# Another order of loads, stores, scores and out products in a fused attention and feed-forward kernel

## The chip, the core and the metric

The kernel runs on one core of a Trainium2 chip. The metric is the device time of one execution in microseconds (us); lower is better. Engines are named as the profile names them: PE is TensorE (its weight loads stand apart as PEld), DVE is VectorE, ACT is ScalarE, POOL is GpSimd, and SP is SyncE, whose queue issues nearly every transfer here.

## What is computed

A linear attention with a decay per head (4 batches, 8 heads, 768 positions, head size 64) is followed by a bilinear feed-forward layer over the 3072 tokens (512 wide, 1536 inside). The reference works in blocks of 64 positions with a running state; the kernel uses blocks of 128.

```python
for b in range(nb):                       # per batch and head
    intra = einsum('bhic,bhjc->bhij', qb, kb) * Dmask
    intra = einsum('bhij,bhjd->bhid', intra, vb)
    inter = einsum('bhid,bhde->bhie', qb * lam_pow, kv_state)
    out[:, :, sl] = intra + inter
    kv_state = lam_block * kv_state + einsum('bhsd,bhse->bhde', kb * rev_pow, vb)
x = out.transpose(0, 2, 1, 3).reshape(3072, 512)
y = ((x @ w_a) * (x @ w_b)) @ w_out       # 512x1536, 512x1536, 1536x512
```

## The kernel before, in words

**Units and groups.** A unit is 128 tokens of one batch with all heads: 24 units, six to a batch. Units 0 to 3 are packed and handled ahead of the loop. The feed-forward part takes the units in eight groups, `GROUPS = (4, 1, 2, 4, 4, 4, 4, 1)`: group 1 is unit 4 alone, group 2 is units 5 and 6, group 3 is units 7 to 10, group 4 units 11 to 14. While group g goes through the feed-forward products, the attention of later units is worked in between.

**Slots.** What is worked in between is written out by hand in `PLAN` (lines 42 to 81): per group a list of (slot, step, unit). The feed-forward code calls `hook(slot)` at fixed points, and each call issues the steps of that slot. Instructions stand on every engine's queue in the order of this program; nothing reorders them. The steps that matter here:

- `PK`, `PV`, `P` (prep, lines 423 to 436): scale k and then q of a unit into one bf16 tile `qk` (line 401; POOL from unit 6 on), and cast v to `vb` (line 420; the engine is listed in `VB_ENG`). For units 7 and up (`DMA_T`) prep also issues a transposing transfer `qkT<-qk` on SP (line 429). Units 4 to 6 are transposed on PE instead (`T`, lines 438 to 446), with a copy on ACT (line 445). After v, `pump()` (line 302) issues the loads of the units that the look-ahead now allows.
- `S` (scores, lines 451 to 482): eight small matmuls `kq<-qkT` (line 457), then two masks on DVE (line 480), or one on DVE and one by way of ACT (lines 471 and 472).
- `O2` (line 571): for two units the products with the state and with the values into `o_ps` (line 497), copied to `xT` by ACT (line 520), and the state update `kvd` (lines 527 and 549). `V` (line 566) is a state update by itself, with a copy into `st` (line 560).
- `W` (line 627): issues one store on SP of a row of results that was kept in SBUF. The five rows of groups 0 and 1 are kept (`o_kept`, line 634) in tiles of `snap_pool`, which has seven buffers. The same pool holds the tiles `u` of line 829, snapshots of PSUM that the feed-forward of groups 3 to 6 needs.
- `WS` (line 260): eight sums of weights, 128x1536 each, ready before group 3 uses them as `wz_a`, `wz_b`. `WS_ENG` names the engine: DVE for 0 to 6 and POOL for 7.
- `X`, `XA`: sums of xT on DVE ahead of group 3 (lines 708 to 722).

**Feed-forward.** Groups 0, 1, 2 and 7 use the plain form (`ffn`): 12 passes of an `a_ps` and a `b_ps` product (line 596), a copy of a on ACT (line 605), the product ab on DVE (line 623); `hook(0)` to `hook(11)` stand behind these passes. Then come, per unit, 12 out products `op<-wo_sb,ab` (line 643), six ahead of a hook and six behind it; then the store and one more hook. Groups 3 to 6 use a form with seven products in place of eight (`ffn_z`, line 748), six passes with three hooks each; its snapshots `u` on ACT and sums `oab` on DVE (lines 777 to 789) stand between products on PE. In group 3 the out products (line 810) follow in `out_plain`, with the hooks 18 to 25.

**Loads.** `pending` (lines 292 to 299) lists all loads in order, for every unit q, k, v. All go through SP's queue in program order, with three buffers each for q, k and v.

Of the kernel before, what the change touches and what calls it, by code (L numbers as in the profile page):

```python
# [22 lines left out]
def _bc(ap, dims):  # L23
# [9 lines left out]
DMA_T = range(7, 24)  # L33
# [71 lines left out]
                        ["act"] * 3))  # L105
SUM_ENG = {(3, 0): 'dve', (3, 1): 'dve', (3, 2): 'pool', (3, 3): 'dve', (3, 4): 'pool', (3, 5): 'pool', (3, 6): 'dve', (3, 7): 'dve', (4, 0): 'dve', (4, 1): 'pool', (4, 2): 'pool', (4, 3): 'pool', (4, 4): 'dve', (4, 5): 'pool', (4, 6): 'pool', (4, 7): 'pool', (5, 0): 'dve', (5, 1): 'dve', (5, 2): 'pool', (5, 3): 'pool', (5, 4): 'dve', (5, 5): 'pool', (5, 6): 'pool', (5, 7): 'dve', (6, 0): 'pool', (6, 1): 'dve', (6, 2): 'pool', (6, 3): 'dve', (6, 4): 'dve', (6, 5): 'pool', (6, 6): 'dve', (6, 7): 'dve'}
XS_ENG = {(3, 0): 'dve', (3, 1): 'dve', (3, 2): 'dve', (4, 0): 'dve', (4, 1): 'dve', (4, 2): 'dve', (5, 0): 'dve', (5, 1): 'pool', (5, 2): 'pool', (6, 0): 'pool', (6, 1): 'pool', (6, 2): 'pool'}
WS_ENG = {0: 'dve', 1: 'dve', 2: 'dve', 3: 'dve', 4: 'dve', 5: 'dve', 6: 'dve', 7: 'pool'}
WO_ENG = {0: 'dve', 1: 'dve', 2: 'pool', 3: 'dve', 4: 'dve'}
CO_ENG = {0: 'pool', 1: 'pool', 2: 'pool', 3: 'dve', 4: 'dve', 5: 'dve'}  # L110

# [2 lines left out]
def kernel(  # L114
# [12 lines left out]
    B, H, S, D = q.shape  # L127
# [3 lines left out]
    d_model, d_ff = moe_w_a.shape  # L131
# [4 lines left out]
    FC = d_ff // 128  # L136
# [123 lines left out]
    def weight_sum(i):  # L260
# [5 lines left out]
        a21, a22 = w[:, 0:2, HF:], w[:, 2:4, HF:]  # L266
        eng = eng_of(WS_ENG[i])
        if j == 0:
# [23 lines left out]
    pending = []  # L292
# [3 lines left out]
    pending += [("o", c) for c in range(4)] + [("q", n0), ("k", n0)]  # L296
    pending += [("o", 4), ("o", 5), ("v", n0)]
    for u in range(n0 + 1, NU):
        pending += [("q", u), ("k", u), ("v", u)]
    used = {"u": 0}  # L300

    def pump():
# [36 lines left out]
    for w, src in (("q", q), ("k", k)):  # L339
# [3 lines left out]
        for c in range(0, HP, n_c):  # L343
            if w == "q":
                t = oab_pool.tile([128, 1024], F32, name="q4", tag="oab")
            else:
                t = snap_pool.tile([128, 512], F32, name="k4", tag="snap")
            t = t[:].rearrange("p (c b x) -> p c b x", c=n_c, b=2)
# [48 lines left out]
    def eng_of(name):  # L397
        return nc.gpsimd if name == "pool" else nc.vector
# [136 lines left out]
    def kv_update(u):  # L535
        if u % NB == NB - 1:
            return
        if u % NB == 0:
            kv_bank()
        kv_mms(kv["ps"], u, range(HP), u % NB == 0)  # L540
# [22 lines left out]
    def piece_S(u):  # L563
        masks(u, scores(u))
# [43 lines left out]
    def a_part(f, xT, gt):  # L608
        return a_copy(half(wa_sb, f, xT, "a_ps", 0, gt), gt)

    def a_parts(fs, xT, gt):
        ps_parts[0] = True
        pss = [half(wa_sb, f, xT, "a_ps", 0, gt // 2) for f in fs]
        a_sbs = []
        for f, ps in zip(fs, pss):
            half(wa_sb, f, xT, "a_ps", gt // 2, gt, ps)
            a_sbs.append(a_copy(ps, gt))
        ps_parts[0] = False
        return a_sbs

    def b_part(f, xT, gt, a_sb, ab):
        ps = half(wb_sb, f, xT, "b_ps", 0, gt)
        nc.vector.tensor_mul(ab[:, f, :gt], a_sb[:, :gt], ps[:, :gt])  # L623
# [7 lines left out]
    def store(row, op, lo, hi, queue=None):  # L631
        if row < g_u0[KEEP_GROUPS]:
            o_sb = snap_pool.tile([128, d_model], F32, name="o_kept", tag="snap")
            nc.scalar.copy(o_sb, op)
            kept.append((row, o_sb))
            return
        o_sb = o_pool.tile([128, d_model], F32, name="o_sb", tag="osb")
        nc.scalar.copy(o_sb[:, lo:hi], op[:, lo:hi])
        (queue or nc.sync).dma_start(out=out_r[row][:, lo:hi], in_=o_sb[:, lo:hi])

    def out_mms(op, ab, t, fs, lo=0, hi=d_model):
        for f in fs:
            nc.tensor.matmul(op[:, lo:hi], lhsT=ab[:, f, t * 128:(t + 1) * 128],  # L643
                             rhs=wo_sb[:, f, lo:hi], start=(f == 0), stop=(f == FC - 1))

    def ffn(u0, n, xT, hook, first, last):
        gt = n * BLK
        ab = ab_pool.tile([128, FC, 512], BF16, name="ab", tag="ab")
        if first:
            for i, cs in enumerate(W_STEPS):  # L650
                nxt = W_STEPS[i + 1] if i + 1 < len(W_STEPS) else ()
                fs = range(w_off[cs[0]] // 128, w_off[cs[-1] + 1] // 128)
                a_sbs = a_parts(fs[:2], xT, gt) if i == 0 else []
                a_sbs += [a_part(f, xT, gt) for f in fs[len(a_sbs):]]
                if i == 0:
                    kv_update(n0 - 1)
                    cast_w("b", cs[1], "both")
                else:
                    for c in nxt:
                        cast_w("a", c, "dve")  # L660
                for n_f, (f, a_sb) in enumerate(zip(fs, a_sbs)):
                    b_part(f, xT, gt, a_sb, ab)
                    hook(f)
                    if i == 0 and n_f == 1:
                        cast_w("a", nxt[0], "dve")
                for c in nxt:
                    cast_w("b", c, "act")
            ops = [ps_bank("op", [128, d_model], F32, hold=True) for _ in range(n)]
            slot = FC
            for c in range(FC // 2):  # L670
                for t in range(n):
                    out_mms(ops[t], ab, t, range(2 * c, 2 * c + 2))
                    if c == FC // 2 - 1:
                        store(u0 + t, ops[t], 0, d_model)
                    hook(slot)
                    slot += 1
            bank["held"].clear()
            return
        for f in range(FC):
            a_sb = a_part(f, xT, gt)  # L680
            b_part(f, xT, gt, a_sb, ab)
            hook(f)
        for t in range(n):
            op = ps_bank("op", [128, d_model], F32, ffn=True)
            if last and t == n - 1:
                for lo, hi in ((0, 256), (256, 384), (384, 512)):
                    if lo:
                        op = ps_bank("op", [128, d_model], F32, ffn=True)
                    out_mms(op, ab, t, range(FC), lo, hi)
                    store(u0 + t, op, lo, hi, nc.scalar if hi == d_model else None)  # L690
                return
            out_mms(op, ab, t, range(FC // 2))
            hook(FC + 2 * t)
            out_mms(op, ab, t, range(FC // 2, FC))
            store(u0 + t, op, 0, d_model)
            hook(FC + 2 * t + 1)
# [318 lines left out]
    for g, n in enumerate(GROUPS):  # L1015
# [6 lines left out]
        def hook(slot, plan=plan):  # L1022
            for name, us in plan.get(slot, ()):
                if name == "C":
                    cast_w("o", us, CO_ENG[us])
                elif name == "PK":
                    prep_k(us)
                elif name == "PV":
                    prep_v(us)
                elif name == "P":  # L1030
                    prep_k(us)
                    prep_v(us)
                elif name == "W":
                    store_kept()
                elif name == "WS":
                    weight_sum(us)
                elif name == "WO":
                    out_sum(us)
                elif name == "SM":
                    ab_sum(*us)  # L1040
                elif name == "H":
                    out_half(*us)
                elif name == "XA":
                    x_add_first(us)
                elif name == "X":
                    x_sums(us)
                elif name == "T":
                    piece_T(us)
                elif name == "S":
                    piece_S(us)  # L1050
                elif name == "VC":
                    kv_copy(us, kv["ps"], KV_ENG[us])
                elif name == "V":
                    piece_V(us)
                elif name == "O":
                    pieces_O((us,))
                elif name == "O2":
                    pieces_O(us)
                else:
                    pieces_O(us[:2], us[2:])  # L1060
# [41 lines left out]
```

## Time and profile before

| what | value |
|---|---|
| median of 3 runs | 224.38 us (224.23 to 226.21) |
| time of the profiled execution | 223.83 us |
| span of the profiled execution (first to last instruction) | 222.1 us |
| PE busy | 213.9 us (96%) |
| DVE, ACT, POOL busy | 165.3, 122.7, 99.8 us |
| transfers | 39.42 MB; read 28.32 MB, written 6.29 MB |
| granted TensorE clock | 1.000 over the span |

The span is 1.7 us shorter than the time of the same execution; the rest lies before the first and behind the last instruction. A busy PE need not be PE at its pace: matmuls are pipelined, so a wait shows best as the distance between the starts of two neighbours. All places are in us from the start of the span.

### The profile page before, as it was taken

The page shows a single profiled execution, that of the slowest core. Times are in us where ns is not written, and L with a number is a line of the kernel's source. Part 1 is how long each engine was busy: PE and PEld are TensorE (multiplying, and loading weights), DVE is VectorE, ACT ScalarE, POOL GpSimd, SP SyncE. Part 2 cuts the span into 40 slices and gives each one's busy share as a digit, 9 for nine tenths or more (in the row PEclk, how much of TensorE's full clock was granted, in tenths as well). Part 3 has the DMA queues.
Part 4 walks back from the last instruction along what each step waited for, and adds up shares of the span by engine and source line. Part 5 has one row for each costly group of instructions (what it writes and reads, how often), then busy time and mean ns, then how long its engine had stood idle before and what let it go on. Part 6 is the DMA issues. An engine that isn't in the chain of part 4 may idle for free.

```text
span 222.1 us, 5601 instructions
## 1 busy us (share of the span) xinstructions
PE 213.9 (96%) x2225; PEld 159.0 (72%) x2235; DVE 165.3 (74%) x272; ACT 122.7 (55%) x249; POOL 99.8 (45%) x95
## 2 busy tenths in 40 slices
PE   7899999999999999999999999899999999999994
PEld 2476444448678657787547888688888888888994
DVE  0994773968798668889888889968688865777540
ACT  3686446038454266775356988776535666543322
POOL 6061004246795175540559559786417722051100
PEclk9999999999999999999999999999999999999999
DMA  4999999999999999999999999652021100112042
GB/s 132 321 265 349 356 387 344 277 216 218 216 204 220 232 174 248 190 275 245 180 248 236 233 201 211 138 101 50 0 88 56 52 0 4 47 47 97 0 145 94
DMA packets 99081, 39.42 MB, mean 177 GB/s; under 512 B 85488, under 2 KB 95088, under 8 KB 99056
## 3 DMA queue, kind: packets, MB, share of 16 engines
q1 hardware_dynamic: 98768, 39.00, 79.8%
q8 instruction: 17, 0.28, 0.6%
q10 hardware_dynamic: 288, 0.07, 0.1%
q14 instruction: 8, 0.07, 0.1%
HBM read 28.32 MB, written 6.29 MB: 156 GB/s over the span
## 4 chain that ended last, share of the span: by engine, by line
PE 67%; DMA 16%; SPq 5%; DVE 5%; ACT 2%; issue 2%; POOL 1%; ACTq 0%; DVEq 0%; POOLq 0%
PE U L748 17%; PE op L870 12%; PE V L748 9%; DMA wst<-in_moe_w_b_dram 8%; PE b_ps L596 5%; PE op L810 5%; PE a_ps L596 5%; PE W L748 4%; PE op L643 3%; DMA kf<-in_k_dram 3%; DMA k<-in_k_dram 3%; PE o_ps L497 3%; PE kq L457 2%; DMA out_dram<-o_kept 2%; SPq L187 1%
## 5 line engine op out<-in xcount | busy, mean ns | idle before, releaser
L829 ACT COPY u<-U 128x512 f32<-128x512 f32 x48 | 28.3, 590 | 16.5 <-PE U L748 16.4
L401 POOL TENSOR_TENSOR qk<-kf,lp_k 128x512 bf16<-128x512 f32 x18 | 19.5, 1084 | 33.7 <-DMA kf<-in_k_dram 18.9
L623 DVE TENSOR_TENSOR ab<-a_sb,b_ps 128x128 bf16<-128x128 bf16 (+2 forms) x48 | 19.2, 417 | 13.6 <-ACT a_sb L605 10.2
L596 PE MATMUL a_ps<-xT,wa_sb 128*128 128x128 bf16 (+2 forms) x198 | 27.6, 267 | 0.5 <-DVE wa_sb L244 0.2
L480 DVE TENSOR_TENSOR m<-kq,lotri 128x512 bf16<-128x512 f32 x40 | 25.6, 682 | 3.1 <-PE kq L457 3.0
L596 PE MATMUL b_ps<-xT,wb_sb 128*128 128x128 bf16 (+2 forms) x192 | 27.5, 272 | 0.2
L756 DVE TENSOR_TENSOR ab<-oab 128x1024 bf16<-128x1024 bf16 x24 | 19.0, 791 | 11.3 <-ACT oab L754 11.1
L401 POOL TENSOR_TENSOR qk<-qf,lp_q 128x512 bf16<-128x512 f32 x20 | 24.8, 1242 | 1.7 <-DMA qf<-in_q_dram 1.7
L605 ACT CAST a_sb<-a_ps 128x128 bf16<-128x128 f32 (+2 forms) x48 | 17.3, 374 | 14.7 <-PE a_ps L596 14.4
L643 PE MATMUL op<-wo_sb,ab 128*128 128x512 bf16 (+2 forms) x114 | 21.8, 334 | 0.5 <-issue 0.3
L596 PEld LDWEIGHTS <-wa_sb 128*128 128x128 bf16 x200 | 16.7, 98 | 6.6 <-issue 0.5
L748 PEld LDWEIGHTS <-wz_a 128*128 128x128 bf16 x192 | 18.2, 98 | 3.9 <-issue 0.9
L748 PEld LDWEIGHTS <-wz_b 128*128 128x128 bf16 x192 | 18.7, 98 | 2.2
L596 PEld LDWEIGHTS <-wb_sb 128*128 128x128 bf16 x192 | 15.8, 98 | 6.2 <-issue 0.2
L748 PE MATMUL U<-xT,wz_a 128*128 128x256 bf16 x96 | 18.3, 272 | 0.0
L748 PE MATMUL U<-xT,wz_b 128*128 128x256 bf16 x96 | 18.3, 272 | 0.0
L520 ACT CAST xT<-o_ps 128x512 bf16<-128x512 f32 (+1 forms) x24 | 12.2, 554 | 10.7 <-PE o_ps L497 10.5
L787 DVE TENSOR_TENSOR oab<-U,u 128x512 bf16<-128x512 f32 x24 | 16.3, 681 | 0.8 <-PE U L748 0.8
L420 POOL CAST vb<-vf 128x512 bf16<-128x512 f32 x14 | 10.2, 730 | 13.8 <-DMA vf<-in_v_dram 13.8
L748 PEld LDWEIGHTS <-wa_sb 128*128 128x128 bf16 x144 | 13.4, 98 | 4.0 <-issue 1.0
L643 PEld LDWEIGHTS <-ab 128*128 128x128 bf16 x120 | 10.1, 98 | 8.5
L754 ACT CAST oab<-U 128x512 bf16<-128x512 f32 x24 | 14.2, 592 | 3.5 <-PE U L748 3.5
(130 smaller groups left out, 453.1 us busy)
## 6 DMA issues: line engine op xcount, KB each, us to landing
vf<-in_v_dram SPq DMA_DIRECT2D x24, 256.0 KB, 4.9
qf<-in_q_dram SPq DMA_DIRECT2D x20, 256.0 KB, 4.6
kf<-in_k_dram SPq DMA_DIRECT2D x20, 256.0 KB, 4.7
out_dram<-o_sb SPq DMA_DIRECT2D x18, 256.0 KB, 2.4
wst<-in_moe_w_a_dram SPq DMA_DIRECT2D x6, 512.0 KB, 8.8
wst<-in_moe_w_b_dram SPq DMA_DIRECT2D x6, 512.0 KB, 9.2
wst<-in_moe_w_out_dram SPq DMA_DIRECT2D x6, 512.0 KB, 10.7
out_dram<-o_kept SPq DMA_DIRECT2D x5, 256.0 KB, 4.3
```

The costliest lines, as they stand in the source:

```text
L401: eng_of(eng).tensor_mul(dst.rearrange("p (c b) d -> p b c d", b=2), x[:].rearrange("p (b c) d -> p b c d", b=2), lp.rearrange("p (b c) o ...
L480: nc.vector.tensor_mul(m, kq[i], lotri_bc)
L596: nc.tensor.matmul(ps[:, lo:hi], lhsT=w_sb[:, s, f * 128:(f + 1) * 128], rhs=xT[:, s, lo:hi], start=(s == 0), stop=(s == KS - 1), skip_gro ...
L605: nc.scalar.copy(a_sb[:, :gt], ps[:, :gt])
L623: nc.vector.tensor_mul(ab[:, f, :gt], a_sb[:, :gt], ps[:, :gt])
L643: nc.tensor.matmul(op[:, lo:hi], lhsT=ab[:, f, t * 128:(t + 1) * 128], rhs=wo_sb[:, f, lo:hi], start=(f == 0), stop=(f == FC - 1))
L748: nc.tensor.matmul(ps[:, k, :], lhsT=wt[:, s, n * 128:(n + 1) * 128], rhs=rhs[i][:, s, :], start=(fresh and k == 0 and s == 0), stop=True, ...
L754: nc.scalar.copy(oab[:, 0], U)
L756: nc.vector.tensor_mul(ab[:].rearrange("p (h i) (t c) -> p h i t c", h=2, t=2)[:, :, n], o5[:, :, :, 0, :], o5[:, :, :, 1, :])
L787: nc.vector.tensor_sub(oab[:, 1], U, v1)
L829: nc.scalar.copy(t, ps)
L870: nc.tensor.matmul(ps[:, t, :], lhsT=lhs[p][:, n, t * 128:(t + 1) * 128], rhs=rhs[:, n, :], start=fresh, stop=True, skip_group_check=True)
```

## The change

In `PLAN`, the sums of weights 5, 6 and 7 move from group 1's slots 0 and 13 to group 1's slot 13 and group 2's slots 9 and 13, and sum 7 moves from POOL to DVE. The transposes of unit 6 now stand ahead of the scores of unit 5. Of the five stores of kept rows, the third moves up behind the first two in group 2's slot 2, and the last two move to group 3's slot 21. The scores of units 11 and 12 and the `O2` behind them move one slot later. The load list has k ahead of q for units 7 to 23. In `ffn`, the 12 out products of a group of one unit are issued as four, hook 12, four, hook 13, four, store; this branch runs for unit 4 alone, since unit 23 leaves by the branch above it.

```diff
     1: [
-        (0, 'PV', 5), (0, 'WS', 5), (3, 'T', 5), (4, 'PK', 6), (6, 'PV', 6), (9, 'P', 7),
-        (11, 'S', 5), (11, 'T', 6), (12, 'S', 6), (13, 'P', 8), (13, 'O2', (5, 6)), (13, 'V', 6),
-        (13, 'WS', 6), (13, 'WS', 7)],
+        (0, 'PV', 5), (3, 'T', 5), (4, 'PK', 6), (6, 'PV', 6), (9, 'P', 7),
+        (11, 'T', 6), (11, 'S', 5), (12, 'S', 6), (13, 'P', 8), (13, 'O2', (5, 6)), (13, 'V', 6), (13, 'WS', 5)],
     2: [
-        (2, 'W', None), (2, 'W', None), (3, 'P', 9), (4, 'V', 7), (4, 'S', 7),
-        (6, 'V', 8), (10, 'PK', 10), (11, 'PV', 10), (11, 'P', 11), (11, 'W', None),
+        (2, 'W', None), (2, 'W', None), (2, 'W', None), (3, 'P', 9), (4, 'V', 7), (4, 'S', 7),
+        (6, 'V', 8), (9, 'WS', 6), (10, 'PK', 10), (11, 'PV', 10), (11, 'P', 11),
         (11, 'S', 8), (11, 'P', 12), (12, 'Q', (7, 8, 9, 10)), (13, 'P', 13),
-        (13, 'W', None), (13, 'V', 9), (14, 'XA', 3), (14, 'O2', (9, 10)), (14, 'X', 3), (15, 'W', None)],
+        (13, 'V', 9), (13, 'WS', 7), (14, 'XA', 3), (14, 'O2', (9, 10)), (14, 'X', 3)],
     3: [
-        (1, 'S', 11), (5, 'S', 12), (8, 'O2', (11, 12)), (10, 'P', 14), (12, 'S', 13),
+        (2, 'S', 11), (6, 'S', 12), (9, 'O2', (11, 12)), (10, 'P', 14), (12, 'S', 13),
...
-        (19, 'P', 16), (19, 'O2', (13, 14)), (20, 'P', 17), (21, 'S', 15), (21, 'P', 18),
+        (19, 'P', 16), (19, 'O2', (13, 14)), (20, 'P', 17), (21, 'S', 15), (21, 'P', 18), (21, 'W', None), (21, 'W', None),
...
-WS_ENG = {0: 'dve', 1: 'dve', 2: 'dve', 3: 'dve', 4: 'dve', 5: 'dve', 6: 'dve', 7: 'pool'}
+WS_ENG = {0: 'dve', 1: 'dve', 2: 'dve', 3: 'dve', 4: 'dve', 5: 'dve', 6: 'dve', 7: 'dve'}
...
     for u in range(n0 + 1, NU):
-        pending += [("q", u), ("k", u), ("v", u)]
+        pending += [("k", u), ("q", u), ("v", u)] if u in DMA_T else [("q", u), ("k", u), ("v", u)]
...
+            if n == 1:
+                out_mms(op, ab, t, range(4))
+                hook(FC)
+                out_mms(op, ab, t, range(4, 8))
+                hook(FC + 1)
+                out_mms(op, ab, t, range(8, FC))
+                store(u0 + t, op, 0, d_model)
+                return
             out_mms(op, ab, t, range(FC // 2))
             hook(FC + 2 * t)
```

In the program's order on SP, the two late stores stand behind the loads of unit 20 and ahead of the last two row stores of group 3 and the transposing transfer of unit 19. Every engine keeps its instructions, but for sum 7, which leaves POOL's queue for DVE's.

6 rows, old and new, of the table PLAN are left out of this document.

## The prediction

> **What bounds the kernel.** I read the page first, then PE's waits, then the chain of waits, then the timeline wherever two neighbours on PE start too far apart.
>
> ```profile
> span 222.1 us, 5601 instructions
> ...
> PE 213.9 (96%) x2225; PEld 159.0 (72%) x2235; DVE 165.3 (74%) x272; ACT 122.7 (55%) x249; POOL 99.8 (45%) x95
> ```
>
> PE is the bound: busy for 96% at a granted clock of 1.000, with neighbouring matmuls of 128, 256 and 512 columns 56, 109 and 216 ns apart. The change removes no matmul, so it can only win where PE waits. PE's own list of waits is short:
>
> ```profile
> PE U L748 <- DVE oab L787: 0.8, 1, 0.8
> ...
> PE V L748 <- ACT u L829: 0.3, 1, 0.3
> ```
>
> The first stands at 141.20, where group 4 ends, and no edit touches it. The second is on the chain:
>
> ```profile
> 83.72 4.32 DMA out_dram<-o_kept
> 88.11 0.59 ACT u L829
> 88.75 0.60 PE V L748 x4
> ```
>
> The third kept row is stored from 83.72 on, lands at 88.03, and only then may ACT's snapshot take its buffer; PE stood behind the snapshot. The list shows 0.3 because it counts a matmul's modelled end; from start to start it is 0.61 where 0.11 is usual: 0.50 lost.
>
> The list shows no shorter wait. Two places on the timeline do. In group 1:
>
> ```profile
> 52.48 1.39 DVE L273 TENSOR_TENSOR wz_b<-wb_sb,wz_b 128x1536 bf16<-128x1536 bf16 x1
> ...
> 53.80 0.67 DVE L623 TENSOR_TENSOR ab<-a_sb,b_ps 128x128 bf16<-128x128 bf16 x3
> ...
> 54.13 0.38 PE L596 MATMUL b_ps<-xT,wb_sb 128*128 128x128 bf16 x4
> ```
>
> Weight sum 5 keeps DVE until 53.8; the products behind it free a PSUM bank late, and PE starts `b_ps` at 54.13, 0.33 behind its neighbour instead of 0.06: 0.27 lost. At the end of group 1:
>
> ```profile
> 60.71 3.09 POOL L275 TENSOR_TENSOR wz_b<-wb_sb 128x1536 bf16<-128x1536 bf16 x1
> 61.39 2.70 DVE L420 CAST vb<-vf 128x512 bf16<-128x512 f32 x1
> ...
> 61.58 0.58 ACT L634 COPY o_kept<-op 128x512 f32<-128x512 f32 x1 [2.01 <-PE op L643]
> ...
> 62.17 1.07 ACT L520 CAST xT<-o_ps 128x512 bf16<-128x512 f32 x2
> ...
> 62.28 0.40 PE L527 MATMUL kvd<-vb,qk 128*128 128x128 bf16 x4
> ...
> 62.80 0.87 PE L596 MATMUL a_ps<-xT,wa_sb 128*128 128x256 bf16 x4
> ```
>
> ACT copies `o_kept` ahead of the two halves of xT, and group 2's first product waits for each half: 0.35 instead of 0.06, then 0.38 instead of 0.11. That is 0.29 + 0.27 = 0.56 lost.
>
> **The change, part by part.**
>
> *Sum 5 leaves group 1's slot 0.* DVE reaches the products 1.39 earlier, and the 0.27 goes. Next to be late would be unit 6's transposes, which now stand first in slot 11: in the kernel before they could start when POOL had scaled q of unit 6 (57.34) and started at 57.90. Without the 0.27 and with unit 5's scores (0.33) behind them, PE wants them at 57.90 - 0.33 - 0.10 - 0.27 = 57.20. If POOL keeps its times, 0.14 or a little more is given back. But POOL's scale at 53.02 took 1.75 beside sum 5, where others take 1.04; without the sum it should be some 0.7 earlier. I take -0.27, bounds -0.27 to -0.10.
>
> *Transposes first, out products in three parts.* The copy `qkT` (1.01 on ACT, begun 0.2 after the last transpose) is ready near 58.9; unit 6's scores want it at 57.20 + 0.45 + 0.33 + 4 x 0.216 + 0.10 = 59.0. Four products more (0.87) bring `O2` at 60.35; unit 6's masks (two, 1.29, from 0.43 behind its scores) end near 60.8 and are wanted near 60.9. `O2` and the state update take 0.80 + 0.23, and the last four products (0.87) bring PE to 62.24, when both halves of xT are copied (near 62.15), since `o_kept` now comes behind them. So the 0.56 goes. `o_kept` ends near 63.0; its bank is wanted by the second `a_ps` at 63.1. Three margins are about 0.1 each: bounds -0.56 to -0.30, and I take -0.56, since each is a margin and not a deficit. Scores and `O2` cost 0.1 each on either side where PE changes to small tiles; their number is the same.
>
> *Third kept store sooner.* It is issued at about 68.7 in place of 83.72 and lands, at the 3.9 to 4.5 us of its kind, near 73, 14 us before its buffer is wanted: -0.50, and behind it the snapshot waits for PE alone. Price: SP's issue (0.36 to 1.10 in the rows) delays what is queued behind: transposing transfers of units 9 and 10 (8 us early for their scores at 76.26), loads of 11 and 12, transfer 11.
>
> *Two later.* The last two leave 95.28 and 96.89 on SP for the place behind unit 20's loads. Their buffers: in the kernel before, group 3's snapshots already turned over in the other five until pass 5; now for pass 5 too. The five sufficed for passes 1 to 4 with no wait of DVE or ACT on a buffer after 88; 0, bounded by one snapshot (0.59). Queued behind them are two row stores and the transfer of unit 19: below.
>
> *k ahead of q.* The 34 loads of units 7 to 23 swap places on SP, two by two. POOL waited 18.9 us in seven waits for kf; it now starts with the load that lands 1.2 us earlier, scales k while q lands, and ends a pair about 1.0 sooner. PE gets nothing: every transposed tile had landed before its scores. Tightest was unit 11 (issued 79.26, landed 84.22, scores 84.85), then 12 (89.00 for 89.77), 19 (131.07 for 132.87).
>
> *Scores 11 and 12 one slot later.* Eight matmuls, two masks and, with `O2`, one state update move past two products (0.87). Unit 11's scores then fall at 84.85 - 0.83 + 0.87 = 84.9. Its transfer: +0.36 to +1.10 for the third store, -0.6 for POOL; its landing 83.6 to 84.7. No wait, bounds 0 to +0.5. `O2` comes one slot nearer to unit 13's scores (3 us of products between), its copies (1.07) fit.
>
> *Sums 5, 6, 7 in their new places.* Sum 5 takes DVE where sum 6 did (1.19). Sum 6 (0.95 to 1.39) falls where DVE idled 0.45 in each pass; unit 8's masks then end up to 0.4 later, where 0.49 was spare before `O2` needed their banks. Sum 7 falls ahead of group 3's sums of xT, where DVE idled 1.59 waiting for ACT's xT at 82.07. POOL is rid of 3.09 us, and the cast beside it (2.70; 0.42 at 67.17) of 2.3. All 0.
>
> [...]
>
> **Sum.** -0.27 - 0.56 - 0.50 = -1.33 us. The profiled execution took 223.83: 222.50 after. Its time lies 0.55 under the median of the runs shown, 224.38; on that scale 223.05, so **223.1 us**.
>
> **Rivals.**
>
> *Unit 11's transfer lands late.* If POOL's gain fails and the store costs SP its 1.10, it lands at 84.22 + 1.10 = 85.3; PE, due at 84.9, waits 0.5: 223.6.
>
> *Sum 7 waits for POOL.* If it loses two scales (2 x 1.04) to POOL, DVE is late by 0.95 + 2.08 - 1.59 = 1.44 for group 3's sums. `z_add` ended 0.76 before its product and the moved scores take 0.33 of that: PE loses 1.0, 224.1. Against it: no DVE row shows two such waits in a row.
>
> *The waits come back later*, at 141.20, and nothing is won: 224.4. Against it: that wait's chain (ACT oab, DVE ab, zab, oab) begins at PE's own products, so it moves with PE.
>
> *Slower: the two late stores hold up unit 19.* In the kernel before its transfer was issued at 125.62 and landed at 131.07; PE now wants its scores at 132.87 - 1.33 = 131.54. If the two stores cost SP 1.10 each and nothing has been won ahead of them, it lands at 133.3: PE waits 1.7, ends at -1.33 + 1.7 = +0.4, 224.8. It turns to slower once unit 19 lands after 132.9. For it: SP waits at 112.67 for a row copied by ACT, so what SP gains from the three stores taken away (1.03 + 1.10 + 0.45) may be lost there. Against it: that row comes 1.33 earlier too, and transfers drain in the meantime.
>
> **Chances.** Sum as worked out 0.66; unit 11 late 0.12; sum 7 behind POOL 0.08; waits come back 0.07; unit 19 late 0.07. The likeliest alone spans 222.5 to 223.6 (the bounds that give back 0.17 + 0.26 + 0.1 on the high side, 0.5 from the wait at 141 or from POOL on the low one). The range 222.4 to 224.8 takes in the third and fourth and reaches to the slower case; it leaves out half of that and the tails: under 2 in 10. About 1% is what a measurement of this kernel can tell from no change: below 222.1 is 0.04 (tail of the first case), above 226.6 is 0.02 (unit 19 with more behind it), within 0.94.
>
> **What would show it.** Right: `b_ps` of pass 4 in group 1 follows 0.06 behind its neighbour; group 2's `a_ps` runs four at 0.11; no ACT wait on `o_kept`; the span near 220.8; PE's list keeps only the wait on oab L787. Wrong: a wait of PEld L457 on a transposing transfer (unit 11 or 19), `o_ps` waiting for a mask in group 1, V's or W's products waiting for DVE at 82 to 86, or a larger wait at 141.

## The result, and the profile after

| | kernel before | changed kernel |
|---|---|---|
| median of 20 executions | 224.16 us (223.50 to 226.21) | 226.18 us (223.42 to 231.32) |
| ratio, without the longest executions | 1 | 1.0044 (95%: 1.0023 to 1.0066) |
| time of the profiled execution | 223.83 us | 225.38 us |
| its span | 222.1 us | 223.6 us |

By the ratio the change made the kernel about 0.4% slower, 1 us; 223.1 us had been forecast. The ratio leaves out executions more than 1.5% above the fastest of their kernel, which are nine of the changed kernel's twenty and none of the kernel before's, while the medians count all and lie 2.0 us (0.9%) apart.

From the page of the changed kernel, its span and its busy time by engine:

```profile
span 223.6 us, 5612 instructions
...
PE 212.8 (95%) x2225; PEld 158.6 (71%) x2235; DVE 167.7 (75%) x273; ACT 122.3 (55%) x249; POOL 97.7 (44%) x94
```

PE has the same 2225 matmuls and a longer span: it waits more. First the three places that the change aimed at. Group 1 on the timeline (start, us, engine, line, operation):

```profile
54.12 0.39 PE L595 MATMUL a_ps<-xT,wa_sb 128*128 128x128 bf16 x4
54.34 0.39 PE L595 MATMUL b_ps<-xT,wb_sb 128*128 128x128 bf16 x4
```

Four products every 0.22: the 0.27 at `b_ps` is gone. The end of group 1:

```profile
61.52 1.07 ACT L519 CAST xT<-o_ps 128x512 bf16<-128x512 f32 x2 [2.17 <-PE o_ps L496]
...
61.87 1.03 PE L642 MATMUL op<-wo_sb,ab 128*128 128x512 bf16 x4
...
62.73 0.60 PE L595 MATMUL a_ps<-xT,wa_sb 128*128 128x256 bf16 x4
62.93 0.58 ACT L633 COPY o_kept<-op 128x512 f32<-128x512 f32 x1 [0.34 <-PE op L642]
...
63.17 0.60 PE L595 MATMUL b_ps<-xT,wb_sb 128*128 128x256 bf16 x4
```

ACT copies both halves of xT while PE works on the last third of the out products; `o_kept` comes behind them; the next four `a_ps` take 0.44, 0.11 each. The 0.56 is gone. And the third kept store, issued at 69.27, landed at 73.29; PE's list of waits has no snapshot behind a store any more. But beside the wait on `oab` that was there before it has a new line:

```profile
PE U L755 <- ACT u L836: 1.3, 2, 1.1
```

The chain of waits (start, us, what) says where it is and what is behind it:

```profile
84.61 0.59 ACT u L836
85.25 0.60 PE U L755 x4
...
134.89 0.44 ACT u L836
135.37 0.60 ACT oab L761
136.03 5.91 DMA vf<-in_v_dram
142.01 0.48 issue
142.48 0.59 ACT u L836
143.12 0.61 PE U L755 x4
```

The load of v of unit 22, issued at 136.03, lands at 141.94. ACT's cast of it stands on ACT's queue ahead of a snapshot, and PE waits for the snapshot. The same two instructions on the timeline, with what ended the idle time ahead of them in brackets:

```profile
141.96 0.62 ACT L417 CAST vb<-vf 128x512 bf16<-128x512 f32 x1 [2.86 <-DMA vf<-in_v_dram]
...
143.12 0.39 PE L755 MATMUL U<-z_mix,wz_a 128*128 128x256 bf16 x2 [1.14 <-ACT u L836]
```

Between starts PE loses 1.30 there. It loses 0.35 at 85.25 (a snapshot again, in the chain above) and 0.21 at 132.61 (scores of unit 19; their transfer landed at 132.56). In the kernel before v of unit 22 was issued at 134.56 and landed at 139.25, and ACT had cast it well before the next snapshot, of 140.43:

```profile
134.56 0.99 SPq L187 DMA_DIRECT2D vf<-in_v_dram  x1
...
139.28 0.62 ACT L418 CAST vb<-vf 128x512 bf16<-128x512 f32 x1
```

The whole account between the two profiled executions: -0.27 - 0.56 - 0.50 as forecast; +0.35 + 0.21 + 1.30 in the new places; together +0.53. The rest is no step of the change on PE: up to the end of group 0, where no edit reaches, the changed kernel's profile is 0.74 later; a mask wait at 50 is 0.12 shorter; from the last landing to the end of the span pass 1.44 in place of 0.98. That makes 1.61; measured 1.55.

The start is chance: the first `o_ps` behind group 0 stands at 49.33 in the first profile of the kernel before and between 49.7 and 50.9 in sixteen others, whatever the kernel. So profiles are compared below by the **stretch** from there to the V product behind `o_ps` in group 6 (174.36): 125.02 before, 125.34 after.

### The profile page after: what moved, and what is told of

It is laid out like the page before. It is cut to its first block, busy times and chain, and to the rows that moved or that the text cites. A ratio compares the mean times of both kernels' runs of the same rounds, so it can differ in the third digit from the quotient of the medians.

```text
span 223.6 us, 5612 instructions
## 1 busy us (share of the span) xinstructions
PE 212.8 (95%) x2225; PEld 158.6 (71%) x2235; DVE 167.7 (75%) x273; ACT 122.3 (55%) x249; POOL 97.7 (44%) x94
## 4 chain that ended last, share of the span: by engine, by line
PE 84%; DMA 8%; SPq 3%; DVE 2%; ACT 1%; issue 1%; ACTq 0%; DVEq 0%
PE U L755 17%; PE op L877 12%; PE a_ps L595 9%; PE b_ps L595 9%; PE op L642 9%; PE V L755 9%; PE op L817 5%; PE W L755 5%; PE o_ps L496 4%; DMA wst<-in_moe_w_a_dram 3%; PE kq L456 3%; DMA vf<-in_v_dram 3%; SPq L186 2%; DMA q<-in_q_dram 2%; PE kvd L526 1%
## 5 line engine op out<-in xcount | busy, mean ns | idle before, releaser
L400 POOL TENSOR_TENSOR qk<-kf,lp_k 128x512 bf16<-128x512 f32 x18 | 20.9, 1164 | 34.1 <-DMA kf<-in_k_dram 18.4
L622 DVE TENSOR_TENSOR ab<-a_sb,b_ps 128x128 bf16<-128x128 bf16 (+2 forms) x48 | 19.7, 418 | 16.4 <-ACT a_sb L604 7.8
L400 POOL TENSOR_TENSOR qk<-qf,lp_q 128x512 bf16<-128x512 f32 x20 | 23.4, 1169 | 1.8 <-DMA qf<-in_q_dram 1.2
L419 POOL CAST vb<-vf 128x512 bf16<-128x512 f32 x14 | 10.9, 777 | 13.9 <-DMA vf<-in_v_dram 13.8
```

The source lines that it names most:

```text
L400: eng_of(eng).tensor_mul(dst.rearrange("p (c b) d -> p b c d", b=2), x[:].rearrange("p (b c) d -> p b c d", b=2), lp.rearrange("p (b c) o ...
```

## The experiments

Each was timed in turn with the kernel before on the same chip. "v22" is the load of v of unit 22, with its time from issue to landing; the next column is the time from its issue to that of unit 21's transposing transfer; then what PE lost near 143.

| run | ratio (95%) | stretch | v22 took | to unit 21 | lost at 143 |
|---|---|---|---|---|---|
| kernel before, first profile | | 125.02 | 4.70 | 4.55 | 0 |
| e5 kernel before again | 0.9996 (0.9965 to 1.0028) | 125.72 | 4.79 | 4.51 | 0 |
| changed kernel | 1.0044 (1.0023 to 1.0066) | 125.34 | 5.91 | 2.70 | 1.30 |
| e11 changed kernel again | 1.0027 (0.9983 to 1.0071) | 126.68 | 5.88 | 2.71 | 1.26 |
| e1 two stores back | 1.0026 (0.9997 to 1.0056) | 125.10 | 4.85 | 3.62 | 0 |
| e2 two stores alone | 1.0026 (0.9996 to 1.0057) | 126.13 | 4.84 | 3.80 | 0 |
| e3 q first | 1.0013 (0.9982 to 1.0043) | 125.37 | 5.88 | 3.22 | 0.89 |
| e4 cast of v22 later | 1.0004 (0.9966 to 1.0042) | 123.96 | 6.34 | 2.70 | 0 |
| e6 scores alone | 0.9991 (0.9963 to 1.0018) | 125.96 | 4.78 | 4.64 | 0 |
| e7 groups 1 and 2 alone | 0.9987 (0.9955 to 1.0018) | 125.29 | 4.83 | 3.45 | 0 |
| e8 stores behind all loads | 1.0189 (1.0139 to 1.0238) | 128.65 | 4.84 | 4.99 | 0 |
| e9 stores ahead of unit 22 | 0.9983 (0.9949 to 1.0016) | 125.27 | 4.96 | 4.75 | 0 |
| e10 change, stores ahead of unit 22 | 0.9981 (0.9949 to 1.0014) | 124.34 | 4.79 | 4.38 | 0 |
| e12 the same, q first | 0.9955 (0.9924 to 0.9986) | 126.52 | 6.43 | 3.17 | 1.53 |
| e15 the same again | 0.9969 (0.9937 to 1.0001) | 125.64 | 5.07 | 4.71 | 0 |
| e13 unit 21's transfer later | none | 132.05 | 4.65 | 11.95 | 0 |
| e14 POOL sum sooner | 1.0109 (1.0069 to 1.0149) | 128.25 | 4.48 | 6.92 | 0 |

**The kernel before, and the changed one, a second time.** No edit.

> The kernel before, unchanged, profiled and timed as if it were a change: how far its own profile and ratio differ from run to run. Ratio 1.000 within 0.002. In the profiles so far PE's first feed-forward product follows its neighbour 0.21 to 0.81 behind the usual distance (near 18) and one shows 1.55 at 21.18; the theory that this start is chance expects another value here, and the waits at 54, 63, 88 and 141 to stand as in the first profile, within 0.1 where they wait for an engine, and by up to 1 us more or less where they wait for a transfer (88). Rival, the start belongs to the kernel: 0.33 at 17.75 as in the first profile.

> The changed kernel unchanged, a second profile and ratio. Theory: v of unit 22 lands at 141.2 or later again and PE loses 0.7 to 1.5 at 143; waits at 85.25 (0.35) and 141 (0.98) stand; none at 54, 63, 88. Stretch 125.0 to 125.6, ratio 1.000 to 1.006. Rival, the 1.30 was chance: no wait at 143, stretch near 124.0.

The start was 49.74 and 50.01: chance, as said. In the kernel before the waits at 55, 64 and 142 stand within 0.1 of the first profile (0.37, 0.57, 0.98), the one for the third store is 0.70 in place of 0.50, and a mask wait of 0.50 came in at 50: the stretch moves by 0.7 with nothing changed. The changed kernel lost 1.26 to unit 22 again, and at transfers 0.59, 0.31 and 0.49 (units 10, 11, 19), so its stretch, 126.68, is above the 125.6 expected. So the 1.30 belongs to the change, and waits for transfers jitter by about half a microsecond.

**Which part makes unit 22 late: the two late stores, or k first?**

The edits of e1 and e3, on the changed kernel; e2 makes the two moves of e1 the other way, on the kernel before:

```diff
-        (13, 'V', 9), (13, 'WS', 7), (14, 'XA', 3), (14, 'O2', (9, 10)), (14, 'X', 3)],
+        (13, 'W', None), (13, 'V', 9), (13, 'WS', 7), (14, 'XA', 3), (14, 'O2', (9, 10)), (14, 'X', 3), (15, 'W', None)],
...
-(21, 'P', 18), (21, 'W', None), (21, 'W', None),
+(21, 'P', 18),
```

```diff
-        pending += [("k", u), ("q", u), ("v", u)] if u in DMA_T else [("q", u), ("k", u), ("v", u)]
+        pending += [("q", u), ("k", u), ("v", u)]
```

> The changed kernel with the last two kept stores put back to group 2's slots 13 and 15. In the profile of the changed kernel PE loses 1.30 at 143.12 (behind ACT's cast of v of unit 22, which landed at 141.94) and 0.21 at 132.61 (unit 19's transfer). Theory, the two late stores delay the loads behind them: both waits go, v of unit 22 lands before 139.5, and what stays is the forecast gain of 1.33 less the 0.35 at 85.25: about 0.98 us under the kernel before, ratio 0.996. Rival, k ahead of q is what delays unit 22 (its v stands last behind q): the waits stay, ratio 1.004 as measured for the change. Rival, the loss lies in the start (0.74) and the tail (0.46), which differ from run to run: the ratio changes by under 0.002.

> The kernel before with nothing but its last two kept stores moved to group 3's slot 21. Theory, these stores alone cost the loads behind them 1.0 to 1.5 us: v of unit 22 lands after 140.4 instead of 139.25, ACT's cast holds a snapshot, PE loses 0.5 to 1.5 near 143; ratio 1.002 to 1.007. Rival, k ahead of q is needed for the loss: no new wait of PE, ratio 1.000 within 0.001.

> The changed kernel with q ahead of k again for all units. Theory (late stores): v stands behind both either way, so v of unit 22 still lands after 141 and PE still loses about 1.3 at 143 and 0.2 at 132.6; the ratio stays at 1.004 within 0.002. Rival (k ahead of q): the waits go, ratio 0.996 to 0.998.

With the two stores back, both waits went, as the theory said, though v22 landed at 141.16 and not before 139.5. With q first the wait for v22 stayed (0.89; v22 took 5.88): k first isn't its cause. The 0.21 for unit 19 went with q first (its transfer landed at 132.26, its scores stood at 132.72), and the ratio, 1.0013, is under the 1.002 to 1.006 expected. And e1's gain did not come (1.0026; 0.996 was expected). It lost 1.21 at a new place, so that PE was late at 143 for this reason too. ACT's timeline of e1:

```profile
100.55 0.59 ACT L836 COPY u<-U 128x512 f32<-128x512 f32 x1 [1.86 <-DMA out_dram<-o_kept]
```

The fourth kept row, issued at 96.02, still lay in the buffer that this snapshot takes. In the kernel before it landed at 99.78, nothing waited, and the buffer went to a later snapshot: buffers go round in the order in which the program gives them back, and the moved scores change that order (in e6, which moves them alone, ACT waited 0.76 for the same store).

e2 missed, though its ratio lies in the range expected: moved alone, the two stores cost PE nothing at 143. PE had lost 1.72 at 91.23 for the third store, which is not moved in e2, and so was late itself. The line in e2's list of waits:

```profile
ACT u L829 <- DMA out_dram<-o_kept: 2.0, 1, 2.0
```

The stores alone do not make the wait; e2's v22 landed 0.7 behind unit 20's scores, the changed kernel's 2.7. It seems to take the late stores and a PE that is sooner.

**Is it the place of the cast on ACT's queue?**

```diff
-(17, 'P', 22), (17, 'S', 20),
+(17, 'PK', 22), (17, 'S', 20),
...
-    5: [(0, 'SM', (4, 1)), (1, 'H', (4, 0)), (1, 'V', 19),
+    5: [(0, 'SM', (4, 1)), (1, 'H', (4, 0)), (1, 'V', 19), (1, 'PV', 22),
```

> The changed kernel with the cast of v of unit 22, and with it the loads of unit 23, moved from group 4's slot 17 to group 5's slot 1, so that it stands on ACT behind the snapshots and not ahead of them; no store moves. Theory, the 1.30 is lost only because the cast stands ahead of a snapshot on ACT's queue: the wait at 143 falls to under 0.3 although v of unit 22 lands as late as before (141 to 142); ratio about 1.3 / 224 lower than the change's, 0.998 to 0.999. Rival, the late load holds PE by another way (POOL's queue, or the scores of units 22 and 23): a wait of about 1 us turns up within 15 us behind it, ratio stays 1.003 to 1.005.

Yes. The timeline of e4, the product that had waited and the cast:

```profile
141.90 0.38 PE L755 MATMUL U<-z_mix,wz_a 128*128 128x256 bf16 x2
...
144.20 0.62 ACT L417 CAST vb<-vf 128x512 bf16<-128x512 f32 x1
```

v22 landed at 142.47, later than in the changed kernel, and PE lost nothing; the stretch is 123.96, 1.38 less. The ratio, 1.0004, is above the 0.998 to 0.999 expected, but its interval takes these in. The 1.30 is the price of one cast that waits for its load ahead of a snapshot on ACT's queue (in the changed kernel cast at 141.96, snapshot at 142.48).

**One part alone: the scores, and groups 1 and 2.**

The edit of e6, on the kernel before. e7 has, of the change, group 1's list, the places and the engine of the sums of weights and the three parts of the out products, and nothing else.

```diff
-    3: [(1, 'S', 11), (5, 'S', 12), (8, 'O2', (11, 12)),
+    3: [(2, 'S', 11), (6, 'S', 12), (9, 'O2', (11, 12)),
```

> The kernel before with nothing but the scores of units 11 and 12 and the out products behind them one slot later. Theory: the product that now stands ahead of the scores waits 0.35 for a snapshot near 85.5, as in the changed kernel at 85.25; and since buffers go round in the order in which the program gives them back, the snapshot of pass 5 gets the buffer of the fourth kept row one snapshot sooner than before, while its store still lands near 99.8: PE loses 0.5 to 1.2 near 101, as it did (1.21 at 101.19) with the two stores put back. Ratio 1.003 to 1.007. Rival, the 1.21 at 101.19 came from the third store or from k ahead of q: only the 0.35 shows, ratio 1.001 to 1.002.

> The kernel before with the edits of groups 1 and 2 on the engines alone: sums of weights 5 to 7 moved, unit 6's transposes first, unit 4's out products in three parts; all stores, loads and scores as before. Theory, transfers set the pace from 60 to 143, and time that PE wins ahead of a wait for a transfer is lost in it: the 0.27 at 54 and the 0.56 at 63 go, and the wait at 88.75 for the third kept store, which lands at the same time, grows from 0.50 to about 1.3; ratio 1.000 within 0.002. Rival, PE's own pace sets the end and the store is issued sooner as PE goes sooner: 0.83 is won, ratio 0.996.

e6 showed the 0.34 at 86.19: that cost belongs to the move of the scores. Eight matmuls of scores had covered a snapshot there. The buffer of the fourth row did come to a snapshot one sooner (ACT waited 0.76 for its store), but PE, 1.7 later there than in e1, lost nothing by it, where 0.5 to 1.2 had been expected; and the ratio, 0.9991, is under all that was expected (1.001 and more).

The chain of waits of e7:

```profile
84.72 4.03 DMA out_dram<-o_kept
...
88.83 0.59 ACT u L836
89.46 0.60 PE V L755 x4
```

The two waits in groups 1 and 2 were gone, and the wait for the third store had grown from 0.50 to 1.40: by this profile, what PE wins ahead of a transfer that does not come sooner it loses there. The profile alone does not prove it. The same wait was 0.50 and 0.70 in the kernel before and 1.72 in e2, where nothing ahead of it is moved, and the interval of e7's ratio takes in a gain of 0.83 (0.9963) as well.

**Can the stores go elsewhere?** Four kernels (one was run twice) moved them behind the loads that PE needs.

e8 starts from e7. e9 is e8 with the last two stores in the third place below. e10 is the changed kernel with its last two stores there; e12 and e15 are e10 with q ahead of k.

```diff
-(11, 'P', 11), (11, 'W', None),
+(11, 'PK', 11), (11, 'W', None), (11, 'PV', 11),
...
-(9, 'P', 23), (9, 'H', (4, 6)),
+(9, 'P', 23), (9, 'W', None), (9, 'W', None), (9, 'H', (4, 6)),
```

```diff
-(17, 'SM', (4, 2)), (17, 'P', 22),
+(17, 'SM', (4, 2)), (17, 'W', None), (17, 'W', None), (17, 'P', 22),
```

> The edits of groups 1 and 2 as above, with q ahead of k and the scores as in the kernel before, and the stores put where they delay no load: the third between the transposing transfer of unit 11 and the loads of unit 13 (some 2.4 us sooner than before, with the same work ahead of the transfer of unit 12), the last two behind the transfer of unit 23, where the queue has run dry. Theory: all three waits that the change aimed at go (1.33), unit 11's transfer keeps its landing (84.2 against scores due near 84.0: up to 0.4 of loss), no wait at 85.25 or 101, v of unit 22 lands under 139.5 since 0.5 MB fewer stand ahead of it, no wait at 143: 0.9 to 1.3 us under the kernel before, ratio 0.994 to 0.996. Rival, the transfers are late by other things than these stores: v of unit 22 lands after 140.5 and PE loses 0.5 or more near 142; ratio 0.998 or above.

> As the kernel with the last two stores behind all loads (edits of groups 1 and 2, third store between the transfer of unit 11 and the loads of unit 13, q first, scores as before), but the last two stores stand ahead of the transfer of unit 22 instead of behind that of unit 23, which held SP until 154 and with it a snapshot. To leave the start out, the stretch from the o_ps product that follows the out products of group 0 (49.33 in the kernel before) to the V product that follows o_ps in group 6 (174.36) is compared: 125.03 and 125.72 us in two profiles of the kernel before, 125.34 in the changed one. Theory: stores land near 147.5, the snapshots that take their buffers are due from 148 on, no wait of 3.5 at 157, no wait at 143: 123.7 to 124.2 us; ratio 0.992 to 0.996. Rival: the gain of 1.33 is again taken by a wait for a transfer behind 100: 124.8 or more, ratio 0.998 or above.

> The changed kernel with nothing but its two late stores moved on, from behind the loads of unit 20 to ahead of the transfer of unit 22. Theory (the two stores are what makes unit 19's transfer and unit 22's v late): the 0.21 at 132.6 and the 1.30 at 143.1 go, v of unit 22 lands by 139.8; the stretch falls from 125.34 to 123.8 to 124.1; ratio 0.994 to 0.997. Rival (the third store, or k first, keeps unit 22 late): v of unit 22 lands after 141 and PE loses 0.7 or more at 143; stretch over 124.6.

> The changed kernel with its two late stores ahead of the transfer of unit 22 and with q ahead of k again. From the last landing to the end of the span every profile shows a time of its own kernel: 0.97 to 0.98 in the kernel before and its two single edits, 1.44 and 1.44 in the changed kernel, 1.42 with the stores moved on, 1.01 and 1.02 with either the stores put back or q first. Theory: without k first this end falls back to 0.97 to 1.20, and k first gives PE nothing: the stretch stays at 124.0 to 124.6 as with the stores moved on alone (124.34), v of unit 22 lands by 140.3, no wait over 0.3 at 132 and 143; ratio 0.994 to 0.998. Rival: k first helps the transfers (POOL starts on the load that lands first), so with q first transfers of units 10 to 12 come later and PE loses 0.5 or more between 76 and 92: stretch 124.8 or more, ratio 0.998 to 1.002.

> The changed kernel with its two late stores ahead of unit 22's transfer and q first, a second time: its first profile fell on the longest of its twelve executions. Theory (gain of 1.33, less 0.35 at 85): ratio 0.993 to 0.998 again; a profile of a usual execution shows v of unit 22 under 5.0 from issue to landing, no wait of PE at 143, and the stretch at 124.0 to 124.6. Rival, the first ratio was luck: ratio 0.998 to 1.001, and v of unit 22 again over 5.8.

e8 went as the theory has it up to 150: v22 landed at 138.79, and nothing over 0.2 was lost at 85, 88, 132 or 143. But SP stood at unit 23's transfer until 154 with the stores behind it. ACT's timeline, and the granted clock by stretches (us, PE busy, clock, share of DMA, GB/s):

```profile
156.55 0.58 ACT L836 COPY u<-op 128x512 f32<-128x512 f32 x1 [3.91 <-DMA out_dram<-o_kept]
```

```profile
153.00:156.50 3.50, 0.85 (x8) 1.00 0.79 222
...
158.00:160.00 2.00, 2.00 (x11) 0.50 0.00 0
...
162.00:164.00 2.00, 2.00 (x20) 1.00 0.00 0
```

The ratio was 1.0189, not the 0.994 to 0.996 expected. PE waited 3.5, and then worked at half clock (0.50 granted from 158 to 160, 1.00 from 162 to 164): 11 products in 2 us, where it has 20 from 162 on.

e10 is the plainest test of the stores. With nothing but the two stores moved on, SP's rows are:

```profile
134.91 1.26 SPq L186 DMA_DIRECT2D vf<-in_v_dram  x1
139.29 1.83 SPq L428 DMA_TRANSPOSE qkT<-qk  x1
...
143.40 1.55 SPq L628 DMA_DIRECT2D out_dram<-o_kept  x2
```

v22 goes out 1.1 sooner than in the changed kernel, took 4.79, and PE lost nothing at 132 or 143; the stretch is 1.0 shorter than in its first profile and 2.3 shorter than in its second. The gain is less than was expected all the same (ratio 0.9981, not 0.994 to 0.997): PE waited 0.34 for unit 10's transfer and 0.39 for a sum of DVE at 85. e9 has the scores where they were, and PE waited 0.55 and 1.56 for the transfers of units 11 and 12; its ratio, 0.9983, is where its rival had it. e8, the same up to there, did not wait. So a PE that is sooner stands at the mercy of those two transfers. The move of the scores, which costs 0.35, gives them one slot more, and that is not always enough: e11 waited 0.31 for unit 11, e15 0.58 for unit 12. e12 is the only one whose interval lies under 1, 0.9955, and e15, the same kernel, gives 0.9969: about 0.4% under the kernel before. Their profiles don't show this as a shorter stretch: e12's execution (226.07) was the longest of its twelve, with a late v22 after a wait of ACT for a row store (3.6, PE 1.19 at 119.4), and e15's lost 0.54 to a mask at 50 and 0.58 to unit 12's transfer. So the stretches expected of e9, e12 and e15 (124.6 at most) were missed, each by waits for transfers or masks between 50 and 121, while the times of e12 and e15 were as expected. k first brings no time that these runs show: 0.9981 with it (e10), 0.9955 and 0.9969 without.

**Why v22 takes longer once it is late.** Over all profiles it took 4.48 to 5.07 where unit 21's transposing transfer was issued 3.45 or more behind it, and 5.88 to 6.43 in the five where that was 2.70 to 3.22.

```diff
-        (13, 'P', 21), (16, 'SM', (4, 0)), (17, 'SM', (4, 2)), (17, 'P', 22),
+        (16, 'SM', (4, 0)), (17, 'SM', (4, 2)), (17, 'P', 21), (17, 'P', 22),
```

> The changed kernel with the scales of unit 21, its transposing transfer and the cast of its v moved behind a POOL sum of group 4 (ab, which ran at 140.37), so that this transfer is issued near 144.5 instead of 138.74; the order on SP and all stores stay. In fourteen profiles v of unit 22 took 4.70 to 4.96 from issue to landing where the transfer of unit 21 was issued 3.45 or more behind it, and 5.88 to 6.43 where it was issued 2.70 to 3.22 behind. Theory, that transfer is what slows it: v of unit 22, issued near 136 to 137 as before, takes under 5.0; relative to the scores of unit 20 (139.19) it lands 1.1 sooner than in the changed kernel, and of the 1.26 to 1.30 that PE lost at 143 to 144 0.2 to 0.4 are left. Rival, v of unit 22 takes longer because it is issued late or beside other traffic: it takes 5.5 or more again, and PE loses about 1.3 at the same place.

v22 took 4.65, as the theory has it, but the run doesn't decide: PE had lost 2.78 at 122 and was late itself, and unit 21's transfer went out 12 us behind v22 (at 149.03, not 144.5), so that PE lost 2.27 at unit 22's scores. The pattern has no test of its own.

The traces keep every packet of the transfers too, and there the delay can be seen. In each of the five profiles, 18 to 24 packets of 256 bytes, the first of which starts 1.68 to 1.76 behind the issue of unit 21's transfer, while v22 is still on its way, take 0.6 to 1.8 each, where the others take some 0.02; v22 lands within 0.13 of their end. In e1, e2 and e7 such packets start just as far behind that issue, but v22 has landed by then; in the other nine profiles no packet of 256 bytes takes over 0.5 while that transfer is on its way. This fits the boundary: 3.2 and 1.7 make 4.9 from v22's issue on, about when it lands by itself, and 3.45 and 1.7 are past that. So what holds v22 comes with unit 21's transfer. Whose packets they are the traces don't say, and why other transposing transfers pass a load without this is open.

That transfer is issued with PE (0.3 to 0.5 ahead of unit 20's scores in all other profiles), v22 with the stream of loads: a PE that is sooner by 1.3 beside loads that are later by 1.5 brings the two together.

**A margin between POOL and DVE.** The loss of 2.78 in e13 was no transfer: DVE's z_mix of 128x512 took 3.30 at 118.69, in place of 0.82, beside a POOL sum of 3.52 that had begun at 118.18. In the changed kernel the two stand like this (DVE and POOL on the timeline):

```profile
117.31 0.82 DVE L733 TENSOR_TENSOR z_mix<-xT 128x512 bf16<-128x512 bf16 x1
...
117.82 3.27 POOL L289 TENSOR_TENSOR wy<-wo_sb 128x1536 bf16<-128x1536 bf16 x1
```

z_mix is 0.51 ahead of the sum. In the kernel before it is 1.69 ahead:

```profile
116.90 1.26 DVE L726 TENSOR_TENSOR z_mix<-xT 128x512 bf16<-128x512 bf16 x1
...
118.59 3.08 POOL L290 TENSOR_TENSOR wy<-wo_sb 128x1536 bf16<-128x1536 bf16 x1
```

With k first it is 0.51 ahead in four profiles of five (here, e1, e4, e10; 1.70 in e11), with q first in one of ten (e2), and 1.67 to 2.83 in the other nine. The likely reason is that k first lets POOL end its scales sooner, so that the sum behind them begins sooner. e14 brings the sum 1 us sooner; the order on SP, PE, DVE and ACT is the changed kernel's.

```diff
-(21, 'P', 18), (21, 'W', None), (21, 'W', None),
-        (24, 'WO', 2),
+(21, 'PK', 18), (21, 'WO', 2), (21, 'PV', 18), (21, 'W', None), (21, 'W', None),
```

> The changed kernel with one POOL instruction, the sum wy of 128x1536 (3.27 us at 117.82), moved ahead of the cast of v of unit 18, about 1.0 sooner; the other four engines have the same order. In the changed kernel DVE's z_mix (0.82) begins at 117.31, 0.51 ahead of that sum; in the kernel before it begins 1.69 ahead. In the profile with unit 21's transfer held back the sum began 0.51 ahead of z_mix, z_mix took 3.30 and ended with it, and PE lost 2.78 behind. Theory, whichever of the two begins second waits for the other's end, and k first has cut the margin from 1.7 to 0.5: here z_mix takes 2.5 to 3.4, PE loses 2.0 to 2.8 near 119, the time is 2 to 3 us above the changed kernel's. Rival, the 3.30 had another cause: z_mix stays under 1.6, PE's start of U from z_mix stays within 0.3 of 118.30 by the same start, and the time stays that of the changed kernel.

e14's timeline, and the granted clock behind it (us, PE busy, clock, share of DMA, GB/s):

```profile
117.25 3.53 POOL L289 TENSOR_TENSOR wy<-wo_sb 128x1536 bf16<-128x1536 bf16 x1
...
117.76 3.57 DVE L732 TENSOR_TENSOR z_add<-xT 128x1024 bf16<-128x1024 bf16 x1
...
121.39 0.61 PE L755 MATMUL W<-z_add,wa_sb 128*128 128x256 bf16 x2 [2.42 <-DVE z_add L732]
```

```profile
121.00:125.00 4.00, 3.61 (x22) 0.58 1.31 171
```

It was z_add and not z_mix that met the sum, 1.53 grown to 3.57; PE lost 2.58, and the clock stood at 0.58 for the next 4 us. The ratio is 1.0109, 0.65% or 1.5 us above the changed kernel's, where 2 to 3 us had been expected; by the medians of all executions e14 is 2.85 and the changed kernel 2.02 above the kernel before. In the profiles of e13 and e14 the DVE instruction that began 0.51 behind the sum ended behind it too, z_mix by 0.29 and z_add by 0.55; z_add takes 0.68 in e7, where POOL is idle as it begins. Neither profile of the changed kernel itself holds this collision; how often its other executions do is open.

The mean granted clock of each execution gives a hint. In e14's profile it is 0.992, which the 4 us at 0.58 account for. It is 0.992 or less in 7 of the 20 executions of the changed kernel and in 17 of 68 over all runs with k first (these 20, e1, e4, e10 and e11), but in 3 of 84 over those with q first (e2, e3, e6, e7, e9, e12 and e15) and in 5 of 148 of the kernel before; e8, e13 and e14, which have long pauses of their own, are not counted. So k first may cost more than the ratios show, by a pause of PE in one execution of four. Those executions have no trace, and what paused in them is not shown.

## Why the prediction was wrong, step by step

- **Sum 5 out of slot 0, -0.27: right.** Gone in every profile with the edit; the bound of -0.10 was not needed.
- **Transposes first and three parts, -0.56: right,** with both copies of xT ahead of `o_kept` as worked out.
- **Third store, -0.50: right in itself.** The price on SP came out higher: unit 11's transfer landed at 85.66, later than the 83.6 to 84.7 given (the low end leaves out the 0.36 that the store takes at least), but its scores stood at 85.78.
- **Scores one slot later, "No wait": wrong by 0.35.** The step asked what the scores wait for, not what they had covered: a snapshot behind them.
- **Two stores later, and the slower rival: the step that failed.** The rival had the place and the mechanism (SP's gain lost in between, a transfer behind the stores late) and a chance of 0.07. It priced unit 19's transfer alone, which was 1.49 later and cost 0.21. Behind it on SP stood v22, 1.47 later, with a cast that stands on ACT's queue ahead of a snapshot; the forecast named neither. Measured: 1.30 for it, and 0.2 for unit 19.
- **k ahead of q, "PE gets nothing": the cost was missed.** The forecast had POOL end a pair 1.0 sooner and took that for harmless. In four profiles of five it brought POOL's long sum from 1.69 to 0.51 behind DVE's last sum of xT; where the sum began 0.51 ahead of z_mix (e13) or z_add (e14), PE lost 2.78 and 2.58.
- **Sum 7 and POOL: the wrong pair.** That sum 7 could lose two scales to POOL was the author's estimate, and the profile does not show it: DVE's sum 7 met nothing (0.95 as priced). What met POOL's long sum was DVE's last sums of xT, z_mix in e13 (3.30 in place of 0.82) and z_add in e14 (3.57 in place of 1.53), and no edit of the change names that pair.
- **The end.** 0.46 more from the last landing to the end was in no step.
- **The range** had each wait at a place of its own. One rival gave all gains back, but at 141.20, behind engines that move with PE; there was no case in which several gains together make PE sooner and the stream of loads, which comes no sooner (v22 out at 136.03, in the kernel before at 134.56), takes them back.

## What to carry to other kernels

When a transfer is moved, follow the queue behind it to the last one that still has a due time, and ask for each what engine handles its landing and what stands behind that instruction: here a cast on ACT, for a load seven transfers behind the first that was looked at, cost six times what that first one did. A gain on the bound engine counts only up to the next wait for something that does not come sooner (in e7's profile 0.83 was won and 0.90 lost, though that wait varies by itself). And an engine that is made sooner off the path can meet another: look at the margin between long POOL and DVE instructions before and after (here z_mix began 1.69 ahead of POOL's sum and then 0.51; beginning 0.51 behind it, z_mix took 3.30 in e13 and z_add 3.57 in e14).

## What the runs showed that was not expected

- Two instructions that trade places on POOL's queue (e14) lengthen the changed kernel by 0.65% with no edit to PE's program, and a pause of PE of 2.4 was followed by a granted clock of 0.58 over the next 4 us.
- From the last landing to the end of the span each kernel has its own time, the same within 0.02 in the three kernels that were profiled twice: 0.97 to 1.03 in the kernel before, e1, e3, e6, e7, e12 and e15; 1.20 in e2, e8 and e9; 1.42 to 1.45 in the changed kernel (twice), e4, e10, e13 and e14. The 0.46 is thus likely a real part of the 1 us. Its cause stays open.
- The first 50 us, the same in all these kernels, vary by 1.5 us between executions.
